# The low-part products of features A done in one piece at a block's end

## The chip, the cores and the metric

The kernel runs on one core of a Trainium2 chip. The metric is the device time of one execution in microseconds (us). The engines of the core work side by side, each through its own list of instructions in order, and wait for each other by semaphores: PE (TensorE) does the matrix products and loads their weights (PEld), DVE (VectorE) and ACT (ScalarE) work on whole tiles, POOL (GpSimd) does some additions and issues some transfers, SP (SyncE) issues the other transfers.

## The reference

A short convolution over the sequence (7 taps per head, the taps softmaxed) is followed by a two-layer network with a squared ReLU:

```python
x_unf = x_pad[:, idx, :].reshape(B, S, K, H, group)
out = np.einsum('hk,bskhg->bshg', w, x_unf)      # x: 8 x 4096 x 192, 7 taps, 8 heads
...
h = x @ w_in                                     # 32768 x 192 @ 192 x 2048
r = np.maximum(h, 0.0)
g = s * (r * r) + b
return (g @ w_out).astype(np.float32)            # 2048 x 192
```

## The kernel before, in words

The 32768 tokens are cut into 32 groups `n` of 1024, and each group into two blocks `j` of 512. The 2048 hidden features are cut into 16 chunks `f` of 128, two to a step: a block has eight steps `p` = 0 to 7 (`NPAIR`). Tokens lie along the free axis. The 192 output features are cut into A (128) and B (64).

Numbers are carried as a high part that the fast fp32 product of PE takes whole and a low part that holds the rest, so a product in full precision is a sum of several products of parts. From group 3 on (`SCALED`) the low part of the squares is a 16-bit tile, scaled by powers of two that are found from the largest input of the group.

**One step** (`for n, j, p in steps`, L972). `first` (L659) makes h of two chunks in PSUM from the split inputs sA, wA, tB, wB: 18 matmuls on 64 rows each. ACT takes the ReLU (L674) and squares it in place (L681). DVE casts the square to its high part qh (L683), and `half_lows` (L701) writes the 16-bit rest into ql. One ql tile holds the rests of two steps; its pool has five buffers (`LAG + 3`). Then `convolve` puts up to two more DVE instructions behind these, from the convolution and the splitting of the next group (L237, L239, L256, L267 to L272).

**The second layer** comes two steps later (`LAG`; a block's first step waits for one more, so that in program order two `first` and then two `second` follow each other at each block's beginning). `second` (L763) multiplies the weights w_out with qh (L773: 4 matmuls for features B, 8 for features A, into the four accumulators of the block) and, from group 3 on, with ql. The products with ql are kept for later: `lows_B` (L758, 16 matmuls) does those of features B for all eight steps at the block's last step, and the loop at L792 to L800 does those of features A (L796) from the list `lows_A`, four matmuls for each step.

**The block's end.** After the last step ACT reads the four accumulators (L810, L813), POOL adds them in pairs (L814, L818), SP moves the upper half of oB to oC, POOL adds that (L823), and SP stores the results.

**The peaks.** In the second block of group n, at step 3, DVE takes the largest absolute input of group n + 2 (`peak`, L207, two reductions). POOL sends the 128 partitions' values to a small place in DRAM (`there`, L151) and fetches them back, broadcast to all partitions (L153). At step 7 `scale` reads them on DVE (m, L161 to L171) and POOL scales the taps. In the program, and so on DVE, `scale` comes behind the last DVE instruction of step 6 and ahead of the cast qh of step 7.

**What sets the order.** The framework lists each engine's instructions by priority in program order, with an estimate of its own of when each is ready; `behind` ties an instruction behind the last one traced on an engine. At run time each engine keeps to its list.

Of the kernel before, what the change touches and what calls it, by code (L numbers as in the profile page):

```python
# [44 lines left out]
def conv_attention_then_squared_relu_mlp(  # L45
# [25 lines left out]
    NPAIR = weights64.shape[0]  # L71
# [72 lines left out]
    def folded(columns):  # L144

        return columns.rearrange("p (a b) -> p b a", a=2)
# [563 lines left out]
    def accumulators(n, j, p):  # L710
        if p == 0:
            acc[n, j] = [ps_o.tile([P, BLK], F32, name=f"acc{k}") for k in (1, 2, 1, 2)[: 4 if n else 2]]
        return acc[n, j]
# [38 lines left out]
    def lows_B(n, j, to, some):  # L752


        for p in some:
            ql = low_halves.pop((n, j, p))
            for k in range(2):
                nc.tensor.matmul(  # L758
                    to[k * DB :][0:DB], halves[1][:, 2 * p + k, :], ql[:, k, :],
                    start=False, stop=p == NPAIR - 1, skip_group_check=True,  # L760
                )

    def second(n, j, p, qh, ql):  # L763
        if (n, j, p) == steps[-1]:
            return last(n, j, qh, ql)
        accs = accumulators(n, j, p)

        ends = [NF - 1, NF - 1 if (n, j) != steps[-1][:2] else NF - 3]

        def both(to, w, f, q, start=False, stop=False):  # L770
            for i in range(2):
                r = slice(i * HB, (i + 1) * HB)
                nc.tensor.matmul(  # L773
                    accs[to + 2 * i], w(f, r), folded(q[r, f % 2, :]),
                    start=start and f == 0, stop=stop and f == ends[i],
                )

        scaled = n >= SCALED
        for f in (2 * p, 2 * p + 1):
            both(1, w_outB, f, qh, start=True, stop=scaled)  # L780
            if not scaled:
                both(1, w_outB, f, ql, stop=True)
        for f in (2 * p, 2 * p + 1):
            both(0, loA, f, qh, start=True)
            both(0, hiA, f, qh)
            if not scaled:
                both(0, hiA, f, ql, stop=True)
        if scaled:
            if p == NPAIR - 1 or (n, j, p + 1) == steps[-1]:
                lows_B(n, j, accs[1], range(p + 1))  # L790
            lows_A.append((p, ql))
            if p % 2 or (n, j, p + 1) == steps[-1]:  # L792
                for f, low in ((2 * k + c, low[:, c, :]) for k, low in lows_A for c in range(2)):
                    for i in range(2):
                        r = slice(i * HB, (i + 1) * HB)
                        nc.tensor.matmul(  # L796
                            accs[2 * i], halves[0][r, f, :], low[r],
                            start=False, stop=f == ends[i],
                        )
                lows_A.clear()  # L800
        if p == NPAIR - 1:
            t0 = n * SUP + j * BLK
            early = (n, j) == (1, 0)

            sb = tok_s[n]
            o = {}
            for k, name in ((1, "oB"), (0, "oA")):
                o[k] = outs.tile([P, BLK], F32, name=name)
                o[k + 2] = outs.tile([P, BLK], F32, name=name + "2", bufs=1)
                nc.scalar.activation(  # L810
                    o[k], accs[k], AF.Identity, scale=sb, bias=0.0 if early else bias[:, k : k + 1]
                )
                nc.scalar.activation(o[k + 2], accs[k + 2], AF.Identity, scale=sb)  # L813
            nc.gpsimd.tensor_tensor(o[1], o[1], o[3], op=ALU.add)  # L814

            oC = outs.tile([DB, BLK], F32, name="oC", bufs=1)
            nc.sync.dma_start(oC, o[1][DB:P])
            nc.gpsimd.tensor_tensor(o[0], o[0], o[2], op=ALU.add)  # L818
            toA, toB = outT[0:P, t0 : t0 + BLK], outT[P:D, t0 : t0 + BLK]
            oB = o[1][0:DB] if early else oC  # L820
            if not early:
                nc.sync.dma_start(toA, o[0])
            nc.gpsimd.tensor_tensor(oB, oC, o[1][0:DB], op=ALU.add)  # L823
            if early:
                unbiased.extend(((o[0], toA, 0), (oB, toB, 2)))
            else:
                nc.sync.dma_start(toB, oB)
            del acc[n, j]
# [14 lines left out]
    def last(n, j, qh, ql):  # L843

        accs = accumulators(n, j, NPAIR - 1)
        sb = tok_s[n]
        uA, uB = upper_sums(accs, sb)
        t0 = n * SUP + j * BLK
        for f in (NF - 2, NF - 1):
            nc.tensor.matmul(  # L850
                accs[1], w_outB(f), folded(qh[:, f % 2, :]), start=False, stop=f == NF - 1
            )
        lows_B(n, j, accs[1], (NPAIR - 1,))
        oB = outs.tile([P, BLK], F32, name="oB")[0:DB]
        nc.vector.scalar_tensor_tensor(
            oB, accs[1][0:DB], sb[0:DB], uB, op0=ALU.mult, op1=ALU.add
        )
        nc.vector.scalar_tensor_tensor(
            oB, accs[1][DB:P], sb[DB:P], oB, op0=ALU.mult, op1=ALU.add
        )  # L860
        nc.sync.dma_start(outT[P:D, t0 : t0 + BLK], oB)
        oA = outs.tile([P, BLK], F32, name="oA")
        for f in (NF - 2, NF - 1):
            for w in (loA, hiA):
                nc.tensor.matmul(
                    accs[0], w(f, slice(0, P)), folded(qh[:, f % 2, :]), start=False, stop=False
                )
        for f in (NF - 2, NF - 1):
            nc.tensor.matmul(
                accs[0], halves[0][:, f, :], ql[:, f % 2, :], start=False, stop=f == NF - 1  # L870
            )
        for k, e in enumerate((nc.scalar, nc.sync)):
            c = slice(k * BLK // 2, (k + 1) * BLK // 2)
            nc.vector.scalar_tensor_tensor(
                oA[:, c], accs[0][:, c], sb, uA[:, c], op0=ALU.mult, op1=ALU.add
            )
            e.dma_start(outT[0:P, t0 + c.start : t0 + c.stop], oA[:, c])
# [93 lines left out]
    steps = [(n, j, p) for n in range(1, NSUP) for j in range(2) for p in range(NPAIR)]  # L971
# [56 lines left out]
    for item in queue:  # L1028
        with in_order(nc.vector):
            second(*item)  # L1030
# [44 lines left out]
```

## Time and profile before

| | |
|---|---|
| median of 3 runs | 2053.38 us (2052.86 to 2054.66) |
| the profiled execution | 2054.64 us |
| its span, first to last instruction | 2052.9 us |
| granted TensorE clock over the span | 1.000 |
| DVE idle ahead of qh, for ACT's square, between 262 and 2020 us | 141.6 us in 113 waits |
| POOL waiting for the peaks to land in DRAM, in the same stretch | 220.1 us in 27 waits, 8.9 at most |
| the peaks' two transfers, median from issue to landing | 8.6 us out, 4.5 us back |

The view by stretches gives PE, DVE, ACT and POOL busy time for each 200 us and counts the instructions; from 400 us on all stretches look alike (PE 199 to 200 us, DVE 171 to 178). The view of waits lists who waited for whom. The timeline lists instructions in order of time, start first, then length, with alike neighbours merged; in brackets stands the engine's idle time just before and what ended it. Matmuls on the two halves of the rows run at the same time, as pairs; a matmul's length in the timeline reaches past the next one's start, since they are pipelined, so only starts are compared.

### The profile page before, as it was taken

What the parts mean: (1) busy time and instruction counts of PE and PEld (TensorE: products, weight loads), DVE (VectorE), ACT (ScalarE), POOL (GpSimd) and SP (SyncE); (2) the same over time, 40 slices, a digit from 0 to 9 for tenths busy, and PEclk for the clock granted to TensorE, in tenths of its full rate; (3) what the DMA queues carried; (4) which work ended last, traced back from release to release, by engine and by line L of the source; (5) the groups of instructions that cost most, each with busy time, mean ns of one, the idle gap of its engine ahead of it and who ended that gap; (6) DMA issues with size and microseconds to landing.
All of it is one profiled execution on the core that took longest, in us unless ns stands there. A gap on an engine that the chain in (4) does not pass through costs nothing.

```text
span 2052.9 us, 43220 instructions
## 1 busy us (share of the span) xinstructions
PE 2042.1 (99%) x18404; PEld 1619.3 (79%) x18404; DVE 1789.1 (87%) x2187; ACT 1331.6 (65%) x1460; POOL 475.8 (23%) x352
## 2 busy tenths in 40 slices
PE   9999999999999999999999999999999999999999
PEld 6789877777777777777777787777777777877776
DVE  9888888888888889888889888898888898888975
ACT  8877866566666665666666656656666666566565
POOL 0013232122231222321222312223212233132210
PEclk9999999999999999999999999999999999999999
DMA  5022222121222222221222222122212222221210
GB/s 196 21 52 77 63 60 63 47 68 45 71 60 50 58 57 58 61 58 49 62 53 71 58 52 58 52 63 60 55 53 60 55 69 59 52 59 47 52 42 19
DMA packets 48561, 121.36 MB, mean 59 GB/s; under 512 B 9200, under 2 KB 9456, under 8 KB 48368
## 3 DMA queue, kind: packets, MB, share of 16 engines
q1 hardware_dynamic: 45824, 114.50, 20.1%
q0 software_dynamic: 2400, 3.97, 1.6%
q8 instruction: 144, 2.36, 0.6%
q14 instruction: 49, 0.40, 0.1%
q10 hardware_dynamic: 144, 0.13, 0.0%
HBM read 35.57 MB, written 25.20 MB: 30 GB/s over the span
## 4 chain that ended last, share of the span: by engine, by line
PE 90%; DVE 4%; DMA 3%; ACT 2%; issue 1%; POOL 0%; SPq 0%; DVEq 0%; POOLq 0%
PE h L659 44%; PE acc L773 31%; PE acc L796 10%; PE acc L758 5%; DMA there<-peak 2%; DMA t<-there 1%; DVE ql L688 1%; ACT q L674 1%; ACT q L681 0%; DVE c L405 0%; DVE t L391 0%; DVE accA L239 0%; DVE qh L683 0%; DVE peak L207 0%; DVE W L411 0%
## 5 line engine op out<-in xcount | busy, mean ns | idle before, releaser
L674 ACT ACTIVATE q<-h 128x1024 f32<-128x1024 f32 x496 | 506.1, 1020 | 585.2 <-PE h L659 570.7
L701 DVE TENSOR_TENSOR ql<-q,qh 128x1024 f16<-128x1024 f32 x464 | 610.9, 1317 | 24.7 <-DVE qh L683 0.5
L681 ACT ACTIVATE q<-q 128x1024 f32<-128x1024 f32 x512 | 543.2, 1061 | 14.3
L773 PE MATMUL acc<-qh,W 64*128 64x512 f32 x3960 | 515.9, 376 | 0.4 <-ACT oA L810 0.3
L683 DVE CAST qh<-q 128x1024 fp32r<-128x1024 f32 x477 | 334.4, 701 | 162.6 <-ACT q L681 156.6
L659 PE MATMUL h<-sA,W 64*128 64x512 f32 x3072 | 461.3, 405 | 2.6 <-DVE W L413 1.7
L773 PEld LDWEIGHTS acc<-qh,W 64*128 64x128 f32 x3960 | 377.2, 186 | 52.7 <-ACT oA L810 0.7
L659 PE MATMUL h<-wA,W 64*128 64x512 f32 x3072 | 416.9, 376 | 0.0
L659 PE MATMUL h<-wB,W 64*128 64x512 f32 x1536 | 413.4, 376 | 0.0
L659 PE MATMUL h<-tB,W 64*128 64x512 f32 x1536 | 413.4, 376 | 0.0
L659 PEld LDWEIGHTS h<-sA,W 64*128 64x128 f32 x3072 | 292.5, 186 | 66.8 <-DVE W L413 2.5
L659 PEld LDWEIGHTS h<-wA,W 64*128 64x128 f32 x3072 | 292.8, 186 | 40.0
L239 DVE SCALAR_TENSOR_TENSOR accA<-xA,taps,accA 128x512 f32<-128x512 f32 x348 | 312.8, 899 | 6.2
L659 PEld LDWEIGHTS h<-tB,W 64*128 64x128 f32 x1536 | 284.7, 186 | 26.7 <-issue 0.2
L773 PE MATMUL acc<-qh,WB 64*128 64x512 f32 x1980 | 304.0, 379 | 1.3 <-DVE qh L683 1.2
L814 POOL TENSOR_TENSOR oB<-oB,oB 128x512 f32<-128x512 f32 x61 | 101.8, 1669 | 874.1 <-ACT oB L810 784.8
L659 PEld LDWEIGHTS h<-wB,W 64*128 64x128 f32 x1536 | 284.7, 186 | 13.5
L796 PE MATMUL acc<-ql,words 64*128 64x512 f16 x1852 | 241.0, 379 | 0.0
L773 PEld LDWEIGHTS acc<-qh,WB 64*128 64x128 f32 x1980 | 186.5, 186 | 32.9 <-DVE qh L683 8.6
L796 PEld LDWEIGHTS <-words 64*128 64x128 f16 x1852 | 72.2, 95 | 119.5 <-issue 64.9
L239 DVE SCALAR_TENSOR_TENSOR accB<-xB,taps,accB 128x512 f32<-128x512 f32 x174 | 161.3, 927 | 3.1
L818 POOL TENSOR_TENSOR oA<-oA,oA 128x512 f32<-128x512 f32 x61 | 113.6, 1862 | 2.8 <-ACT oA L813 2.5
(155 smaller groups left out, 1390.9 us busy)
## 6 DMA issues: line engine op xcount, KB each, us to landing
wA<-sA SPq DMA_DIRECT2D x126, 256.0 KB, 3.4
outT<-oA SPq DMA_DIRECT2D x63, 256.0 KB, 2.4
wB<-tB SPq DMA_DIRECT2D x60, 256.0 KB, 3.4
xA<-in_xA SPq DMA_DIRECT2D x24, 515.0 KB, 3.6
xB<-in_xB SPq DMA_DIRECT2D x32, 259.0 KB, 3.0
oC<-oB SPq DMA_DIRECT2D x61, 128.0 KB, 2.7
outT<-oC SPq DMA_DIRECT2D x60, 128.0 KB, 2.3
words<-in_w SPq DMA_DIRECT2D x7, 768.0 KB, 5.5
```

The costliest lines, as they stand in the source:

```text
L239: nc.vector.scalar_tensor_tensor(acc, src, w[:, k : k + 1], acc, op0=ALU.mult, op1=ALU.add)
L659: nc.tensor.matmul(h[:, i, :], w_in(w, p, chunk[0], rows), folded(chunk[part]), start=start, stop=stop,)
L674: nc.scalar.activation(q, h, AF.Relu, scale=scale)
L681: nc.scalar.activation(q, q, AF.Square)
L683: cast(qh, q)
L688: nc.vector.tensor_tensor(ql, q, qh.bitcast(F32), op=ALU.subtract)
L701: nc.vector.tensor_tensor(ql.rearrange("p f (b a) -> p f b a", a=2), *(v.rearrange("p f (a b) -> p f b a", a=2) for v in (q, qh.bitcast(F3 ...
L758: nc.tensor.matmul(to[k * DB :][0:DB], halves[1][:, 2 * p + k, :], ql[:, k, :], start=False, stop=p == NPAIR - 1, skip_group_check=True,)
L773: nc.tensor.matmul(accs[to + 2 * i], w(f, r), folded(q[r, f % 2, :]), start=start and f == 0, stop=stop and f == ends[i],)
L796: nc.tensor.matmul(accs[2 * i], halves[0][r, f, :], low[r], start=False, stop=f == ends[i],)
L814: nc.gpsimd.tensor_tensor(o[1], o[1], o[3], op=ALU.add)
L818: nc.gpsimd.tensor_tensor(o[0], o[0], o[2], op=ALU.add)
```

## The change

`second` is called once a step. The list `lows_A` collects the steps' low parts; before, it is emptied at every odd step (and at the last step but one of the whole run), so that each two steps their eight matmuls of L796 follow the step's other products. Now the condition is that of `lows_B` above it: the list is emptied once a block, at step 7 (and at the last step but one of the run), so that 32 matmuls of L796 follow the 16 of L758.

```diff
@@ -789,7 +789,7 @@
             if p == NPAIR - 1 or (n, j, p + 1) == steps[-1]:
                 lows_B(n, j, accs[1], range(p + 1))
             lows_A.append((p, ql))
-            if p % 2 or (n, j, p + 1) == steps[-1]:
+            if p == NPAIR - 1 or (n, j, p + 1) == steps[-1]:
                 for f, low in ((2 * k + c, low[:, c, :]) for k, low in lows_A for c in range(2)):
                     for i in range(2):
                         r = slice(i * HB, (i + 1) * HB)
                         nc.tensor.matmul(
                             accs[2 * i], halves[0][r, f, :], low[r],
                             start=False, stop=f == ends[i],
                         )
                 lows_A.clear()
```

The order of the sum in the accumulators of features A changes with it; the operands don't.

## The prediction

> **What bounds the kernel now.** I read the page first, then busy times by stretches of 200 us, then the waits, then one block on the timeline, engine by engine. The first line of the page's busy table:
>
> ```profile
> PE 2042.1 (99%) x18404; PEld 1619.3 (79%) x18404; DVE 1789.1 (87%) x2187; ACT 1331.6 (65%) x1460; POOL 475.8 (23%) x352
> ```
>
> A busy PE may be one that waits, so I look at the rate; in the view by stretches (length, then each engine's busy time and instructions, the granted clock after POOL):
>
> ```profile
> 1000.00:1200.00 200.00, 200.00 (x1838) 158.30 (x1836) 175.44 (x210) 124.27 (x133) 47.95 (x34) 1.00 0.22 57
> ```
>
> The matmuls run in pairs on the two halves of the rows: 1838 of them in 200 us are 0.2176 us a pair. The waits between 262 and 2020 us say how little PE loses (us in total, times, longest):
>
> ```profile
> DVE m L161 <- DMA t<-there: 37.5, 27, 2.3
> ...
> PEld acc L773 <- DVE qh L683: 8.6, 32, 0.9
> ```
>
> So PE works without a break, and the only thing that it now and then waits for is the cast qh on DVE. I write F(p) for the products of L659 of step p (9 pairs), S(p) for those of L773 (6 pairs), A for one piece of L796 (8 matmuls, 4 pairs), B for L758 (8 pairs). One block, from the end of a batch to the end of the next, on PE (start, us):
>
> ```profile
> 826.49 1.04 PE L796 MATMUL acc<-ql,words 64*128 64x512 f16 x8
> ...
> 833.84 1.04 PE L796 MATMUL acc<-ql,words 64*128 64x512 f16 x8
> ...
> 839.89 0.65 PE L773 MATMUL acc<-qh,WB 64*128 64x512 f32 x4
> ...
> 854.65 0.60 PE L773 MATMUL acc<-qh,WB 64*128 64x512 f32 x4
> 855.08 1.03 PE L773 MATMUL acc<-qh,W 64*128 64x512 f32 x8
> 856.04 1.92 PE L758 MATMUL acc<-ql,words 128*64 128x512 f16 x16
> 857.89 1.04 PE L796 MATMUL acc<-ql,words 64*128 64x512 f16 x8
> ```
>
> The rows at 839.89 and 854.65 are S(3) and S(7). The order is A F(2) F(3) S(0) S(1) A F(4) S(2) F(5) S(3) A F(6) S(4) F(7) S(5) A, then F, S(6), F, S(7) with the next block's first two F, B, A: 144 pairs in 857.89 - 826.49 = 31.40 us. S(3) to S(7) holds 68 pairs in 14.76 us, 0.217 us each; so a piece A is 0.87 us and F with S 3.25 us.
>
> Now DVE over the same block. This is a block of the second half of a token group, where DVE also splits accB, takes the peaks of a later group, and, just ahead of qh(7), reads them back as m:
>
> ```profile
> 833.62 1.52 DVE L267 CAST hiB<-accB 128x512 fp32r<-128x512 f32 x1
> ...
> 838.50 0.68 DVE L207 TENSOR_REDUCE peak<-xB 128x1 f32<-128x518 f32 x1
> 839.10 0.69 DVE L683 CAST qh<-q 128x1024 fp32r<-128x1024 f32 x1
> ...
> 842.19 0.69 DVE L683 CAST qh<-q 128x1024 fp32r<-128x1024 f32 x1
> ...
> 845.60 0.69 DVE L683 CAST qh<-q 128x1024 fp32r<-128x1024 f32 x1
> ...
> 848.94 0.69 DVE L683 CAST qh<-q 128x1024 fp32r<-128x1024 f32 x1
> 849.67 1.26 DVE L701 TENSOR_TENSOR ql<-q,qh 128x1024 f16<-128x1024 f32 x1
> 850.85 0.75 DVE L239 SCALAR_TENSOR_TENSOR accA<-xA,taps,accA 128x512 f32<-128x512 f32 x1
> 852.95 0.42 DVE L161 TENSOR_REDUCE m<-t 128x1 f32<-128x256 f32 x1 [1.36 <-DMA t<-there]
> ...
> 853.73 0.68 DVE L683 CAST qh<-q 128x1024 fp32r<-128x1024 f32 x1
> ```
>
> The five casts are qh(3) to qh(7). qh(3) ends at 839.79, 0.10 us before S(3) starts; qh(7) ends at 854.41, 0.24 us before S(7). DVE is 87% busy over the span and looks like slack, but in this block it is just in time at two places. At the second it isn't DVE's own speed: m waits 1.36 us for two transfers that began with the peak's end at 839.18 and were not done before 852.95, 13.77 us later. The mean of the 27 waits is 37.5/27 = 1.39 us, so this block is an average one of its kind, and there are 27.
>
> **The change part by part.** *Work.* The same 32 matmuls of L796 run in each block, with the same operands. Three of four pieces (12 pairs, 2.60 us) leave the steps and go behind B. No DMA and no instruction of another engine is added. PE's sum is unchanged but for switches between the two kinds of operands. One round trip: from 826.49 to 833.84 lie 34 pairs with one such piece, 7.35 us, 0.2162 a pair; 144 pairs at that pitch are 31.13 us, 0.27 under the period. B alone takes 0.12 of it (856.04 to 857.89 is 1.85 for 8 pairs) and the step into it 0.09 (855.08 to 856.04 is 0.96 for 4). That leaves 0.06 for three switches and a wait: I take 0.015 each, between 0 and 0.02, so 58 blocks x 3 x 0.015 = **2.6 us saved**.
>
> *Buffers.* Each ql tile holds two steps; a block fills four of five and B keeps them all to its end already. The first is written again by ql(2) of the next block, which follows F(2), itself behind the whole batch on PE. Nothing new waits there. The accumulators are read out after the batch as before; the next S(0) stays four F and S pieces behind it.
>
> *What the cover was.* Measured from the batch's end, S(2) and S(3) now come 0.87 us earlier, S(4) and S(5) 1.73, S(6) and S(7) 2.60. PE asks for qh sooner; DVE, which runs from qh(2) to qh(6) without a break, doesn't give it sooner. In the first-half blocks, without peaks, that is harmless. The tightest place there is S(4), first DVE, then PE:
>
> ```profile
> 871.55 0.69 DVE L683 CAST qh<-q 128x1024 fp32r<-128x1024 f32 x1
> ```
> ```profile
> 875.41 0.59 PE L773 MATMUL acc<-qh,WB 64*128 64x512 f32 x4
> ```
>
> 3.17 us of slack less 1.73. In the second-half blocks the slack was 0.10 and 0.24, and the change takes 0.87 and 2.60.
>
> *What DVE gains.* hiB at 833.62 took 1.52 us, and POOL's additions explain it:
>
> ```profile
> 827.45 1.72 POOL L814 TENSOR_TENSOR oB<-oB,oB 128x512 f32<-128x512 f32 x1 [25.76 <-ACT oB L810]
> 829.14 1.72 POOL L818 TENSOR_TENSOR oA<-oA,oA 128x512 f32<-128x512 f32 x1
> 833.47 1.38 POOL L823 TENSOR_TENSOR oC<-oC,oB 64x512 f32<-64x512 f32 x1 [2.62 <-DMA oC<-oB]
> ```
>
> L823 ends at 834.85 and hiB at 835.14. In another block hiB was left alone, and the cast ahead of it was not:
>
> ```profile
> 1899.17 1.63 DVE L683 CAST qh<-q 128x1024 fp32r<-128x1024 f32 x1 [1.96 <-ACT q L681]
> 1900.90 1.24 DVE L701 TENSOR_TENSOR ql<-q,qh 128x1024 f16<-128x1024 f32 x1
> 1902.08 0.41 DVE L267 CAST hiB<-accB 128x512 fp32r<-128x512 f32 x1
> ```
>
> hiB is 1.11 us shorter there, qh(2) 0.94 longer. After the change the result oB is ready when B ends, 2.60 us earlier against the batch's end; the transfer of oC and L823 follow it, to about 830.9, right behind L818. qh(2) and ql(2) lie ahead of hiB, 0.73 and 1.18 us from start to start as in the rows at 848.94 and 849.67, so qh(2) starts near 831.7. L823 ends near 832.3 and holds it up: it ends some 0.45 later. Net gain of DVE's chain: 1.11 - 0.45, about **0.6 us**, between 0 (collides as at 1899.17 or stays) and 1.1 (L823 wholly ahead of qh(2)). The value is in the middle, since the shift sets L823 across the start of qh(2).
>
> The Trainium skill (SBUF — State Buffer, "Summary: rules for kernel authors") says that of DVE and GpSimd the second to issue fully blocks until the first is done, when DVE is in a two-port mode. The trace agrees, 1.52 against 0.41 us. By that rule alone a POOL addition moved ahead of qh(2) would free the whole 1.1 us, and the sum below would be 13 us smaller.
>
> *The sum for this block.* Everything of DVE 0.62 earlier, 0.06 us from a cast's end to PE's start (the rows allow 0 to 0.10). S(3) could start at 839.89 - 0.87 = 839.02; qh(3) allows 839.79 - 0.62 + 0.06 = 839.23: PE waits 0.21. S(4) comes at 842.48, qh(4) at 842.26; S(5) at 845.73, just with qh(5); S(6) at 848.98 waits to 849.07. S(7) comes at 852.32, and qh(7) allows 854.41 - 0.62 + 0.06 = **853.85**. In all PE is 853.85 - (854.65 - 2.60) = 1.80 us late at the batch, which cannot be made good, since the batch needs PE alone: 27 x 1.80 = 48.6 us. From it go the waits of before, which fall inside the new ones: 8.6 us at the weight loads, which run ahead of their matmuls, so between 0 and 8.6; I take 5. With the switches: 48.6 - 5 - 2.6 = **+41.0 us**. The profiled execution took 2054.64 us with a span of 2052.9; it becomes 2095.6. It lies 1.26 above the median of the runs, 2053.38, so I forecast **2094.4 us**.
>
> **The rivals.** *(1) The planner fills the waits; faster.* The framework lists each engine's instructions by its own estimate of when they are ready; if it sees S(3) or S(7) late it can set the F behind it first, 9 pairs or 1.95 us, as long as the wait of 1.80 that I find. ACT shows that it can reorder:
>
> ```profile
> 824.37 0.68 ACT L813 ACTIVATE oB<-acc,v 128x512 f32<-128x512 f32 x1
> 824.94 1.06 ACT L681 ACTIVATE q<-q 128x1024 f32<-128x1024 f32 x1
> ```
>
> L813 comes from a later call than this L681. Against it: PE's order above is the program's order throughout, at S(3) with 0.10 us to spare too. It decides once the planner's own estimate makes S late; then neither old nor new waits are left: 2053.4 - 5 - 2.6 = 2045.8. Chance 0.05.
>
> *(2) m goes behind qh(7); no change.* Were m's group not ahead of it, qh(7) could follow accA (ends 851.60) and end at 852.3 - 0.6 = 851.7, before S(7) at 852.05 and more. Only S(3) and S(6) wait, 0.30 in all: 27 x 0.30 = 8.1 against 7.6: 2053.9. The code issues m first and the trace has it so. Chance 0.05. That the pieces don't move at all would give the same time; the new condition leaves no room for it.
>
> *(3) The transfers set less than I think; slightly slower.* With no wait for m at all, the 1.36 us go, S(7) waits 0.44: 27 x 0.44 - 7.6 = +4.3, 2057.7. This needs both transfers faster, and nothing in the change touches them. With what lies between, up to 2070: 0.04.
>
> *(4) The clock drops.* If PE's waits halved the granted clock for the 30 pairs from S(7) to the batch's end, each of the 27 blocks would lose 30 x 0.217 = 6.5 us more: 2094 + 176 = 2270. The stretch above shows a clock of 1.00, with waits of up to 0.9 us in the run; mine reach 1.5. Chance 0.02. The Trainium skill (TensorE: Matmul & The Clock Gate, "Part 1: The HAM clock gate") has the clock halved after an idle window of about 3.4 us; by that rule my waits are too short, and no wait that long stands in these rows.
>
> **How the numbers follow.** My case has 0.81 within 2070 to 2114: no gain of DVE gives 27 x 2.42 - 7.6 = +57.7 (2111), the full gain 27 x 1.32 - 7.6 = +28 (2081), and half a microsecond less or a little more in the transfers moves this by some 12 down or 3 up. Above 2114 lies 0.05, rival 4 in it. The range of 2070 to 2114 leaves 0.19 out. A measurement of this kernel tells about 0.2% (4 us) from no change: faster 0.05, same 0.05, slower 0.90.
>
> **What would show it.** Right: PE's waits for qh L683 rise from 8.6 to some 45 us, nearly all at S(7) in blocks with m; those blocks grow from 31.4 to about 33.1 us and the others stay at 31.3; L796 runs in one stretch of 32; hiB near 0.4 us. Wrong: an F of L659 ahead of S(3) or S(7), or m behind qh(7), or m at less than 13 us from the peak's end, or blocks without peaks that grow.

## The result, and the profile after

The changed kernel takes 2130.39 us (median of 4 runs, 2127.91 to 2134.27) beside 2054.02 us for the kernel before: a ratio of 1.0376, 95% interval 1.0363 to 1.0389. It is slower by 76 us, where +41 was forecast, and 16 us above the top of the range. The sign and the place were right; the size wasn't.

The page of the changed kernel, first line of its busy table (busy us, share, instructions):

```profile
PE 2055.5 (97%) x18404; PEld 1624.1 (76%) x18404; DVE 1750.4 (82%) x2187; ACT 1336.6 (63%) x1460; POOL 434.6 (20%) x352
```

The same 18404 matmuls, now with PE at 97% of a span of 2127.6 us. Of the 74.7 us by which the span grew, 61.3 are idle time of PE; its busy time, in which the ends of matmuls are modelled, holds the other 13.4. The waits of the changed kernel between 262 and 2095 us (who waited for whom, total, times, longest):

```profile
POOL oC L823 <- issue: 170.2, 48, 5.9
...
PEld acc L773 <- DVE qh L683: 92.6, 94, 2.3
PE acc L773 <- DVE qh L683: 62.6, 52, 1.9
DVE m L161 <- DMA t<-there: 36.2, 27, 1.7
```

Two of these lines in the kernel before, between 262 and 2020 us:

```profile
POOL oC L823 <- issue: 33.8, 14, 2.7
```
```profile
PE acc L773 <- DVE qh L683: 1.2, 4, 0.5
```

PE's matmuls wait 62.6 us for the cast qh, where it was 1.2, and the weight loads ahead of them 92.6, where it was 8.6. m waits as long as before, 36.2 us against 37.5. And one line has grown fivefold: POOL's addition L823 waits 170 us in 48 places for nothing that the profile names. Where the trace has the landing of oC's transfer, L823 starts 0.12 to 0.16 us behind it, so it is that transfer that it waits for.

One block of the second half, PE's timeline, from a batch to the end of the next (start, length, idle before):

```profile
846.41 1.92 PE L758 MATMUL acc<-ql,words 128*64 128x512 f16 x16
848.26 3.63 PE L796 MATMUL acc<-ql,words 64*128 64x512 f16 x32
...
864.65 0.70 PE L773 MATMUL acc<-qh,WB 64*128 64x512 f32 x4 [1.11 <-DVE qh L683]
...
879.51 0.70 PE L773 MATMUL acc<-qh,WB 64*128 64x512 f32 x4 [1.52 <-DVE qh L683]
...
881.00 1.92 PE L758 MATMUL acc<-ql,words 128*64 128x512 f16 x16
```

L796 now comes as one stretch of 32 behind L758. The rows at 864.65 and 879.51 are S(3) and S(7), and there PE waits, as forecast. From batch to batch this block takes 881.00 - 846.41 = 34.59 us; before it was some 31.4.

Taken from the starts of L758 in the timeline, for the whole run: the 27 second-half blocks in which peaks are taken went from 31.51 to 34.34 us on the mean, the 29 others from 31.35 to 31.31. 27 x 2.83 - 29 x 0.04 = 75 us: all of the loss lies in the 27 blocks.

DVE and POOL in the same block:

```profile
856.03 2.23 DVE L683 CAST qh<-q 128x1024 fp32r<-128x1024 f32 x1 [4.56 <-ACT q L681]
...
859.53 0.43 DVE L267 CAST hiB<-accB 128x512 fp32r<-128x512 f32 x1
...
863.32 0.68 DVE L207 TENSOR_REDUCE peak<-xB 128x1 f32<-128x518 f32 x1
863.92 0.68 DVE L683 CAST qh<-q 128x1024 fp32r<-128x1024 f32 x1
```

```profile
855.18 1.27 POOL L823 TENSOR_TENSOR oC<-oC,oB 64x512 f32<-64x512 f32 x1 [4.26 <-issue]
856.42 1.28 POOL L818 TENSOR_TENSOR oA<-oA,oA 128x512 f32<-128x512 f32 x1
```

hiB fell from 1.52 to 0.43 us, as expected. But qh(2), the first row, rose to 2.23 us (1.80 on the mean of the 27 blocks, 0.73 before): it met not one addition but two. L818 used to run first, in DVE's gap behind the batch. Here it stands behind L823, which waits for the transfer of oC; then both run back to back from 855.18 to 857.70, and qh(2) ends 0.56 us behind the second. The batch's end lies near 851.73 (848.26 and 16 pairs at 0.217), so the peaks end 12.27 us behind it, where the prediction's block had 839.18 - 827.36 = 11.82 and the forecast 11.2.

POOL's instructions were listed in another order by the framework: before, L814, L818, L823; now, in all 27 blocks, L814, L823, L818. The working instructions of PE (apart from the moved pieces), DVE and ACT stand in the same order as before; SP's has the stores of oC and oA exchanged, as their sources are.

### The profile page after: what moved, and what is told of

Same layout as the page of the kernel before. It is cut to its first block, busy times and chain, and to the rows that moved or that the text cites. A ratio compares the mean times of both kernels' runs of the same rounds, so it can differ in the third digit from the quotient of the medians.

```text
span 2127.6 us, 43216 instructions
## 1 busy us (share of the span) xinstructions
PE 2055.5 (97%) x18404; PEld 1624.1 (76%) x18404; DVE 1750.4 (82%) x2187; ACT 1336.6 (63%) x1460; POOL 434.6 (20%) x352
## 5 line engine op out<-in xcount | busy, mean ns | idle before, releaser
L701 DVE TENSOR_TENSOR ql<-q,qh 128x1024 f16<-128x1024 f32 x464 | 617.8, 1331 | 24.7 <-PE h L659 0.5
L683 DVE CAST qh<-q 128x1024 fp32r<-128x1024 f32 x477 | 362.9, 761 | 275.9 <-ACT q L681 271.7
L659 PE MATMUL h<-sA,W 64*128 64x512 f32 x3072 | 428.3, 384 | 2.6 <-DVE W L413 1.7
L773 PE MATMUL acc<-qh,WB 64*128 64x512 f32 x1980 | 309.1, 385 | 62.7 <-DVE qh L683 62.6
L814 POOL TENSOR_TENSOR oB<-oB,oB 128x512 f32<-128x512 f32 x61 | 100.7, 1651 | 828.8 <-ACT oB L810 739.4
L239 DVE SCALAR_TENSOR_TENSOR accA<-xA,taps,accA 128x512 f32<-128x512 f32 x348 | 262.2, 754 | 6.2
L773 PEld LDWEIGHTS acc<-qh,WB 64*128 64x128 f32 x1980 | 179.1, 186 | 115.0 <-DVE qh L683 93.1
L796 PE MATMUL acc<-ql,words 64*128 64x512 f16 x1852 | 209.9, 377 | 0.0
L796 PEld LDWEIGHTS <-words 64*128 64x128 f16 x1852 | 85.4, 94 | 119.8 <-issue 23.9
L810 ACT ACTIVATE oA<-acc,bias,v 128x512 f32<-128x512 f32 x57 | 44.5, 780 | 158.1 <-PE acc L796 158.1
```

Of the source, the lines that this page charges most:

```text
L239: nc.vector.scalar_tensor_tensor(acc, src, w[:, k : k + 1], acc, op0=ALU.mult, op1=ALU.add)
L659: nc.tensor.matmul(h[:, i, :], w_in(w, p, chunk[0], rows), folded(chunk[part]), start=start, stop=stop,)
L683: cast(qh, q)
L701: nc.vector.tensor_tensor(ql.rearrange("p f (b a) -> p f b a", a=2), *(v.rearrange("p f (a b) -> p f b a", a=2) for v in (q, qh.bitcast(F3 ...
L773: nc.tensor.matmul(accs[to + 2 * i], w(f, r), folded(q[r, f % 2, :]), start=start and f == 0, stop=stop and f == ends[i],)
L796: nc.tensor.matmul(accs[2 * i], halves[0][r, f, :], low[r], start=False, stop=f == ends[i],)
```

## The experiments

**Theory 1**: the loss is PE's earlier demand against a fixed chain on DVE and through the peaks' transfers, in 27 blocks, plus some 1.1 us a block because POOL's flipped order makes that chain later instead of earlier. **Theory 2**: the order is harmless, and something else (slower transfers, DVE as a whole, the longer batch itself) makes up the difference. The kernels ran in three sets, each beside its own runs of the kernel before, which agree within 0.6 us between the sets and lie 2.4 to 2.9 us under those of the first result. "Block" is the mean length of the 27 second-half blocks, from batch to batch in the profiled run; the others take 31.31 us wherever the pieces are done at the end, 31.32 by fours and 31.35 otherwise, but for e11_spread_again and e7_spread (31.33 and 31.32).

| run | us | before | ratio, 95% interval | block, us |
|---|---|---|---|---|
| e1_pool_order | 2083.31 | 2051.12 | 1.0159 (1.0142 to 1.0176) | 32.65 |
| e2_scale_late | 2088.31 | 2051.12 | 1.0183 (1.0168 to 1.0199) | 32.81 |
| e3_both | 2057.91 | 2051.12 | 1.0034 (1.0021 to 1.0047) | 31.72 |
| e7_spread | 2048.54 | 2051.12 | 0.9988 (0.9978 to 0.9997) | 31.35 |
| e4_after_again | 2111.71 | 2051.65 | 1.0293 (1.0278 to 1.0309) | 33.64 |
| e5_by_four | 2104.91 | 2051.65 | 1.0260 (1.0244 to 1.0277) | 33.54 |
| e6_before_pool_flipped | 2081.18 | 2051.65 | 1.0144 (1.0128 to 1.0161) | 32.48 |
| e7_before_scale_late | 2051.16 | 2051.65 | 0.9998 (0.9989 to 1.0007) | 31.40 |
| e8_spread_without_change | 2050.31 | 2051.12 | 0.9997 (0.9988 to 1.0006) | 31.35 |
| e9_peak_earlier | 2055.68 | 2051.12 | 1.0018 (1.0010 to 1.0027) | 31.44 |
| e10_before_peak_earlier | 2053.18 | 2051.12 | 1.0010 (1.0001 to 1.0019) | 31.35 |
| e11_spread_again | 2049.02 | 2051.12 | 0.9987 (0.9978 to 0.9996) | 31.34 |

**POOL's old order in the changed kernel.**

```diff
-            nc.gpsimd.tensor_tensor(oB, oC, o[1][0:DB], op=ALU.add)
+            with behind(nc.gpsimd):
+                nc.gpsimd.tensor_tensor(oB, oC, o[1][0:DB], op=ALU.add)
```

> The changed kernel with one order restored: POOL adds oA (L818) ahead of oC, as before the change, by tying the oC addition behind it. Theory 1: in the changed kernel POOL's list has the oC addition ahead of the oA addition, so the oA addition is held until oC's transfer lands, both fall on qh(2) (2.23 us instead of 0.69), and DVE's chain to qh(3), to the peaks and to m is 0.5 us later instead of 0.6 us earlier, in 27 blocks: with the order restored about 1.2 us of each of those blocks goes, 2095 us (2087 to 2103), qh(2) at most 1.7 us, S(3) waiting 0.2 to 0.4 us. Theory 2: POOL's order is harmless and the waits are longer because the transfers of the peaks or DVE itself got slower: 2122 us or more.

2083.31 us, below the range of theory 1. POOL and DVE of a second-half block in this run (L823 is L824 here):

```profile
898.70 1.71 POOL L814 TENSOR_TENSOR oB<-oB,oB 128x512 f32<-128x512 f32 x1 [24.66 <-ACT oB L810]
902.83 1.27 POOL L818 TENSOR_TENSOR oA<-oA,oA 128x512 f32<-128x512 f32 x1 [2.42 <-ACT oA L813]
904.51 1.28 POOL L824 TENSOR_TENSOR oC<-oC,oB 64x512 f32<-64x512 f32 x1 [0.41 <-POOL oA L818]
```

```profile
905.50 0.85 DVE L683 CAST qh<-q 128x1024 fp32r<-128x1024 f32 x1 [4.54 <-ACT q L681]
...
907.63 0.44 DVE L267 CAST hiB<-accB 128x512 fp32r<-128x512 f32 x1
```

L818 runs in the gap, L824 just ahead of qh(2), which takes 0.85 us. On the mean of the 27 blocks the peaks end 11.17 us behind the batch: 0.64 us earlier than in the kernel before (11.80), against 12.25 in the changed kernel. hiB takes 0.89 us less than before the change on the mean, qh(2) and ql(2) together 0.40 more. Part of the time below the range is something else: the next experiment.

**The changed kernel once more.** In the first set the peaks' transfers were shorter than in the profile of the changed kernel. So it was run again in the second set, with no edit.

> The changed kernel once more, beside the runs that follow. In the first four experiments the two transfers of the peaks took less: POOL waited 208 us for them in all instead of 219, and from the peak's end to m lay 13.1 us instead of 13.8. Theory 1a: that comes with the chip, and the loss goes with it: 27 x 0.7 = 19 us less loss where the transfers are as short as in those runs, so +57 us, and +76 where they are as long as in the first profile. Theory 2: it comes with the edits; then +76 us whatever the transfers take.

2111.71 us, +60.1 where theory 1a had +57. From the peak's end to m lie 13.12 us on the mean, in the first profile 13.75: 27 x 0.63 = 17 us, where the losses differ by 16. POOL's waits for the first of the two transfers, changed kernel first, then this run:

```profile
POOL t L153 <- DMA there<-peak: 219.4, 27, 8.6
```
```profile
POOL t L153 <- DMA there<-peak: 206.7, 27, 8.0
```

So between these two measurements of one kernel the length of the transfers goes into the time about one for one. All further experiments are compared with 2111.71 us, not with 2130.39: e1_pool_order lies 28 us under it, and its block is 1.0 us shorter (27 x 1.0 = 27). Whether the chip sets the length of the transfers, the runs can't say.

**The flip alone, in the kernel before.**

```diff
-            nc.gpsimd.tensor_tensor(o[0], o[0], o[2], op=ALU.add)
...
+            nc.gpsimd.tensor_tensor(oB, oC, o[1][0:DB], op=ALU.add)
+            with behind(nc.gpsimd):
+                nc.gpsimd.tensor_tensor(o[0], o[0], o[2], op=ALU.add)
...
-            nc.gpsimd.tensor_tensor(oB, oC, o[1][0:DB], op=ALU.add)
```

> The kernel before with nothing moved on PE; only POOL's addition oC is put ahead of the addition oA, as the planner does in the changed kernel. Theory 1: the two additions meet DVE one after the other behind the batch, the chain to qh(3), the peaks and m is about 1 us later in the 27 blocks and the slack of 0.1 and 0.2 us is gone: +15 to +27 us. Theory 2 (the order is harmless): within 4 us.

+29.5 us, a little over theory 1's range and far from theory 2. DVE, POOL and PE of a block:

```profile
649.93 1.51 DVE L267 CAST hiB<-accB 128x512 fp32r<-128x512 f32 x1
651.36 1.50 DVE L271 CAST tB<-accB 64x512 fp32r<-64x512 f32 x1
```
```profile
649.62 1.54 POOL L820 TENSOR_TENSOR oC<-oC,oB 64x512 f32<-64x512 f32 x1 [4.14 <-issue]
651.12 1.46 POOL L822 TENSOR_TENSOR oA<-oA,oA 128x512 f32<-128x512 f32 x1
```
```profile
657.22 0.70 PE L773 MATMUL acc<-qh,WB 64*128 64x512 f32 x4 [0.86 <-DVE qh L683]
```

The second addition holds up tB by 1.1 us (1.50 for 0.41), the chain is 1.1 us late (peaks at 12.90), the slack of 0.1 us at S(3) is gone, and the block is 1.08 us longer than the 31.40 us of e7_before_scale_late, which has POOL's old order and ran in the same set: 27 x 1.08 = 29. No matmul was moved. An order on an engine that is 23% busy costs the kernel 1.4%.

**m behind qh(7), and both edits together.** `scale` is called behind the casts of step 7 instead of ahead of them.

```diff
-            elif p == 7:
-                with behind(nc.vector):
-                    ahead[n + 2].scale()
...
             queue.append((n, j, p, *low))
+        if j == 1 and p == 7 and SCALED <= n + 2 < NSUP:
+            with behind(nc.vector):
+                ahead[n + 2].scale()
```

> The changed kernel with m and the three instructions behind it put behind the cast qh(7) and ql(7) on DVE; POOL's order as in the changed kernel. Theory 1: the wait at S(7) for the transfers of the peaks is most of the loss; it goes, and only the wait at S(3) of about 1.3 us stays in 27 blocks: 27 x 1.3 = 35, less 7 for the old waits and switches, about 2082 us (2074 to 2090). Theory 2 (DVE as a whole is too slow for the new pace, wherever m stands): 2110 us or more, with waits spread over S(4) to S(7).

> Both edits: POOL's old order and m behind qh(7). Theory 1: S(3) waits 0.2 to 0.4 us in 27 blocks and nothing else does: 27 x 0.3 = 8, less 7: 2055 us (2049 to 2062), no loss left. Theory 2: 2100 us or more.

2088.31 and 2057.91 us, both within theory 1's ranges. In the first, DVE at the end of a block:

```profile
670.39 0.69 DVE L683 CAST qh<-q 128x1024 fp32r<-128x1024 f32 x1
671.11 1.25 DVE L701 TENSOR_TENSOR ql<-q,qh 128x1024 f16<-128x1024 f32 x1
672.29 0.40 DVE L161 TENSOR_REDUCE m<-t 128x1 f32<-128x256 f32 x1
```

qh(7), ql(7), and then m without a wait: qh(7) is done before S(7) asks for it, and only S(3) still waits. Against 2111.71 us the late m is worth 23 us, POOL's order 28, both 54; they add up, as waits at two places on one path do. Theory 2 falls: with two orders put right, the pieces at the end cost 6.8 us.

**In the kernel before, m late.**

> The kernel before with m put behind qh(7) and ql(7). Theory 1: it takes away the few waits at S(7) that the kernel before has (0.16 us a block on the mean): 0 to 5 us faster. If it is faster by more, part of what the other experiments with this edit gain isn't owed to the change.

0.5 us less, no difference that can be told. The 23 us are therefore owed to the change: before it, PE did not ask for qh(7) early enough to notice.

**Half of the change.** `p % 4 == 3` in the condition: two pieces of 16 matmuls a block.

> The pieces are done every four steps instead of every two or once: PE asks for S(2) to S(3) and S(6) to S(7) 0.87 us earlier than before the change, for S(4) and S(5) no earlier. POOL's list is flipped here too. Theory 1: PE waits 1.2 us at S(3) in 27 blocks, the same total up to S(7): +27 us (20 to 34) over the kernel before. Theory 2 (POOL's order plays no part): 0.8 us at S(3): +16 us. A theory by which the length of the last batch itself costs would give a third of the change's loss, or none.

+53 us, nearly the whole loss, and neither theory's number. Half of the change doesn't cost half. DVE and POOL show why:

```profile
655.16 0.69 DVE L683 CAST qh<-q 128x1024 fp32r<-128x1024 f32 x1 [2.81 <-ACT q L681]
655.96 3.48 DVE L701 TENSOR_TENSOR ql<-q,qh 128x1024 f16<-128x1024 f32 x1
```
```profile
655.82 1.28 POOL L823 TENSOR_TENSOR oC<-oC,oB 64x512 f32<-64x512 f32 x1 [4.02 <-issue]
657.06 1.26 POOL L818 TENSOR_TENSOR oA<-oA,oA 128x512 f32<-128x512 f32 x1
```

```profile
664.47 0.70 PE L773 MATMUL acc<-qh,WB 64*128 64x512 f32 x4 [1.78 <-DVE qh L683]
```

POOL's list is flipped here too, and with the shorter batch its additions come a little later against DVE: they miss qh(2), and in this block they hit ql(2), which takes 3.48 us instead of 1.26 (ql(2) is held up in 14 of the 27 blocks, the instructions behind it in most others). The peaks end 12.88 us behind the batch on the mean, 0.6 more than in the changed kernel. S(3), asked for as early as in the full change, waits 1.78 us here, 1.7 on the mean. I had assumed the collision of the full change.

**The peaks a step earlier.** `elif p == 2` for `elif p == 3` at the call of `peak`, in the changed kernel and in the one before.

> The changed kernel with the peaks taken a step earlier, ahead of qh(2) instead of qh(3), into the gap in which DVE waits for the first square behind the batch; m stays ahead of qh(7), POOL's list flipped. Theory 1: 1.9 us leave the chain ahead of qh(3) and the transfers are long done at m, so both waits go: 2046 to 2052 us, with up to 0.3 us at S(3) where POOL's additions meet DVE. A theory by which the longer batch or the later low parts cost by themselves leaves 2070 us or more.

> The kernel before with the same move of the peaks. Theory 1: it had next to no waits to lose: within 3 us of the kernel before, and 1 to 3 us slower than the changed kernel with the same move.

2055.68 and 2053.18 us. The blocks do what theory 1 says, 31.44 and 31.35 us, and the loss of 60 us is down to 4.6. But the first is slower than expected and slower than the second. In both the batch that opens the 27 blocks ends 3 us later than in the kernel before (263.1 and 263.3 us against 260.2): the move has a price in the stage ahead, which I hadn't considered. The rest, 27 x 0.09 = 2 us between the two, is lost in e9_peak_earlier mostly in 10 of the 27 blocks, in steps of at most 0.3 us spread over S(4) to S(7). PE's matmuls show no wait there, their weight loads this one between 262 and 2040 us:

```profile
PEld acc L773 <- DVE qh L683: 7.4, 30, 0.6
```

In these blocks DVE brings each qh only just in time. What makes it later there than in the 17 others, the runs don't show.

**A version without the waits.** Both orders put right, and in the first halves from group 4 on three DVE instructions of the convolution behind each even step instead of two, so that the second halves have less ahead of qh(3). The third expectation is for the same version with the pieces every two steps again.

```diff
-            convolve(3 if n == 1 else 3 - p % 2 if (n, j) == (2, 1) else 2)
+            convolve(3 if n == 1 else 3 - p % 2 if (n, j) == (2, 1) or (j == 0 and n > SCALED) else 2)
```

> Both edits, and in the first-half blocks, which have 3 us of slack in the changed kernel, three DVE instructions of the convolution are put behind an even step instead of two, so that the second-half blocks have that much less to do ahead of qh(3). Theory 1: no wait of PE for qh is left, blocks of both halves take 31.3 us, 2046 us (2044 to 2052), under the kernel before. Theory 2: as slow as the third kernel or slower.

> The fastest kernel so far, beside the three others on one chip: 2 to 4 us faster than the kernel before, an interval of its ratio that lies under 1.

> The fastest kernel so far (POOL's old order, m behind qh(7), convolution spread to the first halves) without the change: the pieces are done every two steps again. Theory 1: no wait for qh in either, so the two differ by three switches between kinds of operands in each of 58 blocks, 0.04 us a block: this one 2 to 3 us slower than with the change, and 0 to 2 us faster than the kernel before. If it is as fast as with the change, the change saves nothing.

2048.54 and 2049.02 us, 2.1 to 2.6 us under the kernel before, and 2050.31 without the change. Waits of this version on DVE and on PE between 262 and 2040 us:

```profile
DVE m L161 <- DMA t<-there: 80.2, 26, 4.8
```
```profile
PE acc L773 <- DVE qh L683: 0.5, 1, 0.5
```

m now waits 80 us, more than twice as long as in the changed kernel, and PE hardly at all: the same wait costs nothing once no cast that PE needs stands behind it. With and without the pieces at the end differ by 1.3 us where 2 to 3 were expected. By blocks it is the 0.04 us expected, 31.31 against 31.35 in 26 of the 27 with peaks and in nearly all others; but three blocks of e11_spread_again are longer (32.24, 31.81 and 31.41 us) and take back 1.4 us more than the one long block without the change (31.47). By time alone the two intervals (0.9978 to 0.9996 and 0.9988 to 1.0006) overlap, so what the change saves once its waits are gone is seen in the blocks, not settled by the clock.

## Why the prediction was right and wrong

- **PE works without a break and has slack for qh only in the first halves**: right. Blocks without peaks went to 31.31 us, and the whole loss lies in the 27 with peaks.
- **Switches save 2.6 us**: right in size, 0.04 us a block in the 29 that show nothing else; in the 27 with peaks there was nothing to save (below).
- **No wait for ql's buffers**: right; no such line appears among the waits.
- **PE asks 0.87, 1.73 and 2.60 us earlier, and S(3) and S(7) pay**: right as to the places. e2_scale_late takes the wait at S(7) away alone, e3_both nearly both. The shares were wrong: not nearly all of PE's wait is at S(7) but 33 of the 62.6 us, and 30 at S(3), because the chain comes late and not early.
- **The transfers set m**: right. m comes 13.75 us behind the peaks' end, 13.79 before; and where it was 13.12 the loss was 16 us smaller.
- **"Net gain of DVE's chain ... about 0.6 us, between 0 ... and 1.1"**: wrong, and this is the step that failed. The prediction let L823 "follow ... right behind L818", that is, it took POOL's order as given. The framework put L823 first, and the chain came 0.45 us later (12.25 against 11.80). The term was mis-signed by 1.07 us a block, 27 x 1.07 = 29 us of the 35 that are missing. With the order restored the chain is 0.64 us earlier, the value forecast.
- **The other 6 us**: the trace lets the mean block of the changed kernel be added up along the chain: the peaks' end behind the batch, m behind that, m to the end of qh(7), from there to S(7), S(7) to L758, and the batch itself. Measured, 12.25 + 13.75 + 1.46 + 0.07 + 1.49 + 5.32 = 34.34 us, the block's length; in the prediction's numbers, 11.20 + 13.77 + 1.46 + 0.06 + 1.39 + 5.32 = 33.20. Besides the failed term only the way from S(7) to L758 differs, 27 x 0.10 = 3 us: where S(7) has waited, its second pair starts 0.32 us behind the first instead of 0.22. The last 3 us are deductions that were too large: where this chain alone sets the block, saved switches can't shorten it (27 x 0.045 = 1 us), and the kernel before had only 27 x (31.51 - 31.40) = 3 us of old waits beyond the block that the sum starts from, not 5.
- **The range** ended at no gain. A loss on this term wasn't thought of, though the rows already showed qh(2) at 1.63 us under one addition, and rival 1 said that the planner reorders; I looked for it on PE alone, where it would help.
- **Rivals**: the planner didn't fill PE's waits (the order of F and S is unchanged). m stayed ahead of qh(7). Moved behind it by hand, with POOL's order put right too, it left a loss of 6.8 us where rival 2 had 0.5; with POOL's new order it left 37, and PE waited at S(3) alone. The transfers were 0.6 us shorter in later runs, a part of what rival 3 needed, and took 16 us off the loss. The clock stayed at 0.999 with single waits of up to 1.9 us.

## What to carry to other kernels

Work taken out of the steps of a bound engine speeds those steps up, and every producer must keep the new pace step by step: compare each hand-over's slack with the shift at that place, not the engines' busy shares. Work on an engine that is mostly idle can still set the time, through what it blocks; when a change moves a wait or a result, compare the order of all engines' instructions before and after. A read-back that takes 14 us belongs behind the instruction that another engine is waiting for, not ahead of it; where nobody waits, as in the kernel before, the place makes no difference.

## What was not expected of the hardware

A DVE instruction that meets two POOL additions in a row is often not let in between them: qh(2) took 2.23 us above and ql(2) 3.48, where alone they take 0.69 and 1.26, and they ended 0.56 and 1.12 us behind the end of the second. The Trainium skill (SBUF — State Buffer, "Summary: rules for kernel authors") has the second of DVE and GpSimd to issue blocked until the first is done, where DVE is in a two-port mode or has two inputs in SBUF; hiB beside one addition, 1.52 us in the kernel before, agrees, and the two rows show that the blocked one may miss its turn before the next addition too. It isn't always so. Of the 21 casts qh that started beside the first of the pair in the changed kernel, 18 ended 0.55 us behind the second, but 3 ended 0.65 behind the first, and the second addition then took 1.82 us instead of 1.28. In e6_before_pool_flipped hiB ended at 651.44, 0.28 us behind the first addition, when the second had already begun. What decides it, the runs don't show.

The same two small transfers, of 1 KB out and a broadcast back, took 13.75 us from the peaks to m in the first profile of the changed kernel and 13.12 in the second set's run of it, and its loss was 16 us smaller there.
